# Attention into a soft mixture of experts: logits in two halves, a new order for the last batch, two more resident weight quarters

## The chip, the cores and the metric

One core of one Trainium2 chip runs the whole program. The metric is the device time of one execution in microseconds; below it is the median of three runs of the kernel before.

## What is computed

The input is `q`, `k`, `v` (8 batches, 8 heads, 576 positions, 64 channels) and forget gates `f`. Causal attention with a decay from the running sum of `log f` gives `x`, 4608 tokens of 512 channels. A soft mixture of 8 experts with 4 slots each follows:

```python
logits = x @ phi                              # 4608 x 32
d = softmax of logits over all tokens         # dispatch
slot_input = d.T @ x                          # 32 slots x 512
h = maximum(slot_input[e] @ w1[e], 0); slot_out[e] = h @ w2[e]
c = softmax of logits over the 32 slots       # combine
out = c @ slot_out                            # 4608 x 512
```

The softmax over tokens runs over the batches with a running maximum for each slot; the sums so far (`acc`) are scaled down when a batch raises it.

## The kernel before

**Loop.** The order of all instructions is written out by hand. The main loop takes one pair of heads in each step `g` from 1 to 31 (four pairs make a batch). `s1` and `tops` take row maxima of the scores two heads ahead, `mturn` and `mrows` bring them into a row of the query tile (ACT copies them to `mr`, a DMA on SP's queue moves them to `YA`, and the first `s2` matmul of the next step needs them), `s2` makes the scores again with maximum and decay subtracted, `expo` exponentiates on ACT, `causal` masks on POOL, `s3` multiplies with the values at the end of the step, and `norm` divides. `px` and `xcopy` transpose the former pair's result into a channel tile `XT`, 144 columns for each quarter of the tokens (128, and 16 of the ninth half block).

**Mixture inside the loop.** With `b, w = divmod(g - 4, 4)`, the mixture of batch `b` runs one batch behind the attention. At the end of the step with `w = 0`, `logits` makes 16 products (four pairs by four groups of 32 partitions of one PSUM tile; each is two matmul instructions). At `w = 1`, `weigh` copies them to SBUF (ACT, L386), `spread` copies the ninth block's logits to `TK` (POOL, L393), `mgroup` takes the maximum of each partition (DVE, L399), `mcast` transposes the maxima, `tokens` makes two transposes of 128 x 128 (L434), `tcopy`, `highest` and `mine` follow. At `w = 2`, `shift`, `shift2` (an exponential) and `dispatch` (L461), whose result DVE adds to `acc` (L467). `combine` prepares the second softmax. PSUM tiles named `s`, `lg`, `tk` and `ds` share three buffers; `ring` is another list of three banks, taken in turn.

**Closing stretch.** After step 31 come the last pair's `norm`, its transposes (`xt`, L334, L351), `dispatch` of batch 6, the last logits, `weigh`, `spread`, `mgroup`, `tokens`, `mcast`, `shift`, `dispatch` of batch 7, and a transpose of `acc` to `slT`. Between them stand `split` and `cols`, which cut the combine weights into a rounded part and a rest (ACT L678, DVE L680) and transpose them (PE L688) into `cT` (ACT L694). `cols(0)`, `cols(1)` and `cols(2)` run here; `cols(3)` runs among the experts.

**Experts and output.** `STEPS` orders first products (`mlp1`, L900) and second products (`mlp2`, L937) of the experts. Their weights come in 64 quarters of 512 KB. The first `NRES = 23` have SBUF tiles of their own and are loaded in loop steps 5 to 27 (`wload`). The others go through `wstream` into tiles as they fall free: query and key tiles from step 28 on, other tiles in steps 29 to 31 and in the closing stretch, and then the first quarters' own tiles. `block` multiplies `cT` with the slots' outputs (L1015), copies on ACT and DVE and writes `out` by DMA (L1021), first for the left half of the channels, between the last `mlp2`. Every DMA is issued in order on SP's queue.

Of the kernel before, what the change touches and what calls it, by code (L numbers as in the profile page):

```python
# [17 lines left out]
NS = NE * SPE  # L18
# [10 lines left out]
NRES = 23  # L29
# [43 lines left out]
def attn_softmoe(ctx: ExitStack, tc: tile.TileContext, qk, v, f, phi, w1, w2, cst, out):  # L73
# [6 lines left out]
    cs = const.tile([P, 258], F32, name="cs")  # L80
    ident, srep, ones = cs[:, 0:128], cs[:, 128:256], cs[:, 256:258]
# [18 lines left out]
    RAW = [per.tile([P, 2, S], F32, name=f"RAW{i}") for i in range(3)]  # L100
# [3 lines left out]
    XT = [per.tile([P, S], F32, name=f"XT{i}") for i in range(NPAIR)]  # L104
    V = per.tile([P, 2, NBLK, 130], F32, name="V")
    slT = per.tile([P, P], F32, name="slT")
    LD = const.tile([P, NBLK, NS], F32, name="LD")

    LGM = const.tile([P, 274], F32, name="LGM")
    LG, TK = LGM[:, 2:146], LGM[:, 146:274]  # L110
    most = [LGM[:, n : n + 1] for n in range(2)]
    fin = const.tile([P, 8], F32, name="fin")

    mk = const.tile([P, NE], F32, name="mk")
    MT = [const.tile([P, 2 * NBLK], F32, name=f"MT{i}") for i in range(3)]
# [220 lines left out]
    def channels(g):  # L336
        return XT[g % NPAIR].rearrange("p (j c) -> p j c", c=144)

    def last(g, pm, copy):

        for h in range(2):
            rows = slice(64 * h, 64 * h + 64)
            copy(channels(g)[rows, :, 128:144], pm[rows, 64 * h : 64 * h + 64].rearrange("p (j c) -> p j c", c=16))

    def xt(g, ts, copy):

        pm = turn()
        for n, t in enumerate(ts):
            turned(pm[:, 128 * n :], g, t)
        n = len([t for t in ts if t < 4])  # L350
        copy(channels(g)[:, ts[0] : ts[0] + n, 0:128], pm[:, 0 : 128 * n].rearrange("p (j c) -> p j c", c=128))  # L351
        if 4 in ts:
            last(g, pm[:, 128:256], copy)

# [40 lines left out]
    def mgroup(b):
        if not batch(b):
            return
        st["mb", b] = small.tile([P, 2], F32, name=f"mb{b}", tag="mb")
        nc.vector.tensor_reduce(st["mb", b][:, 0:1], LGM[:, 0:146], axis=AX.X, op=ALU.max)  # L399

    def mcast(b):

        if not batch(b):
            return
        pm = turn()[:, 0:128] if b == B - 1 else pv[0][:, 325:453]
        nc.tensor.transpose(pm, st["mb", b][:, 0:1].broadcast_to([P, P]), ident)
        st["cast"] = pm
# [102 lines left out]
    nc.sync.dma_start(cs, cst[:, 0:258])  # L510
# [152 lines left out]
    nc.vector.memset(TK, 0.0)  # L663
    nc.vector.memset(LGM[:, 0:2], -1.0e30)
# [33 lines left out]
    for g in range(1, NG):  # L698
# [188 lines left out]
    hs = XT[0][:, 0:512].rearrange("p (n c) -> p n c", n=2)  # L887
# [57 lines left out]
    for e, k in STEPS[:-4]:  # L945
# [140 lines left out]
```

## Time and profile before

| | us |
|---|---|
| median of three runs | 385.4 |
| lowest and highest | 384.98, 385.47 |
| the profiled execution, its own time | 385.63 |
| its span in the trace | 383.9 |
| PE busy | 361.9 (94%) |
| DVE, ACT, POOL busy | 281.6, 264.5, 262.4 |

The span runs from the first to the last instruction in the trace; 1.7 us of the execution's time lie outside it. Busy times are sums over the whole span, and a busy PE is not one at its peak. The mean granted clock of TensorE is 0.985 of full speed. The DMA queue of the hardware moved 92.73 MB.

### The profile page before, as it was taken

To read this page: it belongs to the slowest core of one execution; us is meant where nothing else is said; L and a number is where in the kernel's file an instruction comes from. 1 tells how busy PE (TensorE), PEld (TensorE's weight loads), DVE (VectorE), ACT (ScalarE), POOL (GpSimd) and SP (SyncE) were. 2 spreads that over 40 slices of the span, in tenths; PEclk is the share of its full clock that TensorE was granted. 3 is DMA by queue.
4 is the path that set the end of the run, shared out by engine and by line. 5 is a ranking of instruction groups with operands and counts; after the bars stand their busy time and mean duration, and the time that the engine had idled before them with its cause. 6 is when DMAs were issued, how large, how long until landed. Compare 5 with 4: busy or idle time off the path is not lost.

```text
span 383.9 us, 15067 instructions
## 1 busy us (share of the span) xinstructions
PE 361.9 (94%) x5777; PEld 323.2 (84%) x5777; DVE 281.6 (73%) x1133; ACT 264.5 (69%) x670; POOL 262.4 (68%) x381
## 2 busy tenths in 40 slices
PE   7999999999999999999998999999999998999850
PEld 6788999999999999999998999999999885444640
DVE  8987787889788978897888788888887543312551
ACT  8868787878787878787877787878786554011441
POOL 8797888878887888788877888888788821000000
PEclk9999999999999999999999999999999999999985
DMA  7766757677868777787777777777755999999998
GB/s 221 201 158 171 192 150 229 196 236 219 251 189 239 229 241 203 205 245 218 217 216 215 215 212 223 218 216 217 219 163 153 279 358 376 381 408 409 359 360 352
DMA packets 34052, 93.68 MB, mean 244 GB/s; under 512 B 4169, under 2 KB 9983, under 8 KB 33981
## 3 DMA queue, kind: packets, MB, share of 16 engines
q1 hardware_dynamic: 33980, 92.73, 77.1%
q8 instruction: 45, 0.74, 0.8%
q14 instruction: 27, 0.21, 0.1%
HBM read 63.93 MB, written 9.73 MB: 192 GB/s over the span
## 4 chain that ended last, share of the span: by engine, by line
PE 83%; DMA 6%; ACT 3%; DVE 3%; POOL 1%; issue 1%; SPq 0%; DVEq 0%; ACTq 0%; POOLq 0%
PE pv L308 23%; PE ring L275 14%; PE ring L276 12%; PE s L225 12%; PE pv L334 4%; PE pv L937 3%; PE lg L380 2%; PE ds L461 2%; PE pv L900 2%; PE more L900 2%; DMA YA<-mr 2%; DMA WB<-WA 1%; ACT PTS L282 1%; DMA out<-p 1%; PE more L937 1%
## 5 line engine op out<-in xcount | busy, mean ns | idle before, releaser
L282 ACT ACTIVATE PTS<-ring 128x320 f32<-128x320 f32 (+2 forms) x256 | 118.5, 502 | 47.4 <-PE ring L276 39.8
L238 DVE CUSTOM_DVE_ANT_0 s<-s,mask 128x320 f32<-128x320 f32 (+4 forms) x320 | 137.9, 451 | 6.1 <-PE s L225 1.1
L275 PE MATMUL ring<-YA,WA 67*128 67x320 f32 (+9 forms) x384 | 121.7, 329 | 1.6 <-DMA YA<-mr 1.6
L276 PE MATMUL ring<-YB,WB 128*128 128x320 f32 (+4 forms) x384 | 110.7, 296 | 0.0
L308 PE MATMUL pv<-V,PTS 128*64 128x65 f32 x3200 | 102.3, 223 | 0.9 <-POOL PTS L290 0.9
L308 PEld LDWEIGHTS pv<-V,PTS 128*64 128x64 f32 x3200 | 97.2, 138 | 4.1 <-POOL PTS L290 1.3
L225 PE MATMUL s<-WA,YA 66*128 66x288 f32 (+9 forms) x384 | 96.8, 306 | 1.4 <-ACT WA L545 0.5
L204 POOL TENSOR_TENSOR WB<-RAW,WB 64x576 fp32r<-64x576 f32 x64 | 90.5, 1415 | 7.2 <-DMA WB<-WA 2.3
L209 POOL TENSOR_TENSOR YB<-RAW,YA 64x576 fp32r<-64x576 f32 x64 | 89.7, 1421 | 2.5
L275 PEld LDWEIGHTS ring<-YA,WA 67*128 67x128 f32 (+3 forms) x384 | 69.0, 181 | 7.2 <-DMA YA<-mr 1.9
L276 PEld LDWEIGHTS ring<-YB,WB 128*128 128x128 f32 (+1 forms) x384 | 69.9, 182 | 0.0
L225 PEld LDWEIGHTS s<-WA,YA 66*128 66x128 f32 (+1 forms) x384 | 64.1, 190 | 5.9 <-DVE LGM L238 1.3
L238 DVE DVE_READ_ACCUMULATOR2_ANT MT<- 128x1 f32 x372 | 52.6, 141 | 0.0
L293 POOL TENSOR_SCALAR_AFFINE_SELECT PTS<-PTS 128x128 f32<-128x128 f32 (+1 forms) x128 | 31.5, 268 | 25.8 <-ACT PTS L282 24.2
L178 ACT CAST WA<-RAW 64x576 fp32r<-64x576 f32 x64 | 40.2, 669 | 7.9 <-DMA RAW<-in_qk 7.2
L290 POOL TENSOR_SCALAR_AFFINE_SELECT PTS<-PTS 128x384 f32<-128x384 f32 x64 | 33.4, 523 | 15.5 <-ACT PTS L282 8.4
L183 ACT CAST YA<-RAW 64x576 fp32r<-64x576 f32 x64 | 40.3, 670 | 0.5
L238 DVE CUSTOM_DVE_ANT_0 s<-s,mask,MT 128x288 f32<-128x288 f32 x62 | 32.6, 526 | 9.0
L334 PE MATMUL pv<-cs,X 128*128 128x128 f32 x155 | 37.0, 272 | 0.0
L327 DVE TENSOR_TENSOR X<-pv,rl 128x320 f32<-128x320 f32 (+1 forms) x65 | 31.6, 487 | 2.4 <-DMA V<-in_v 0.3
L322 DVE TENSOR_SCALAR rl<-pv 128x5 f32<-128x5 f32 x64 | 10.5, 164 | 27.7 <-PE pv L308 27.4
L369 ACT COPY XT<-pv 128x128 f32<-128x128 f32 (+1 forms) x93 | 24.9, 306 | 0.0
(190 smaller groups left out, 342.7 us busy)
## 6 DMA issues: line engine op xcount, KB each, us to landing
w<-in_w SPq DMA_DIRECT2D x46, 512.0 KB
RAW<-in_qk SPq DMA_DIRECT2D x31, 576.0 KB
V<-in_v SPq DMA_DIRECT2D x32, 325.0 KB
WB<-WA SPq DMA_DIRECT2D x31, 288.0 KB
YB<-YA SPq DMA_DIRECT2D x31, 288.0 KB
p<-in_w SPq DMA_DIRECT2D x7, 512.0 KB
out<-RAW SPq DMA_DIRECT2D x12, 256.0 KB
out<-p SPq DMA_DIRECT2D x5, 512.0 KB
```

Source lines behind the costliest of these rows:

```text
L178: nc.scalar.copy(WA[g % 3][0:64, S * h : S * h + S], RAW[g % 3][64:128, h])
L183: nc.scalar.copy(YA[g % 3][0:64, h, 64:640], RAW[g % 3][0:64, h])
L204: nc.gpsimd.tensor_tensor(t[0:64], RAW[g % 3][64:128, h], t[64:128].bitcast(F32), op=ALU.subtract)
L209: nc.gpsimd.tensor_tensor(YB[g % 2][64:128, h], RAW[g % 3][0:64, h], YA[g % 3][0:64, h, 64:640].bitcast(F32), op=ALU.subtract)
L225: nc.tensor.matmul(t[:, o : o + w], ya[0:m, h, 128 * blk : 128 * blk + 128], wa[0:m, j0 : j0 + w], start=True, stop=True)
L238: nc.vector.tensor_tensor_reduce(out=t[:, o : o + w], in0=t[:, o : o + w], in1=mask[:, m0 : m0 + w], scale=1.0, scalar=top if n == 3 else ...
L275: nc.tensor.matmul(o, wa[0:m, j0 : j0 + n], ya[0:m, h, 64 + i0 : 64 + i0 + w], start=True, stop=False)
L276: nc.tensor.matmul(o, wb[:, j0 : j0 + n], yb[:, h, i0 : i0 + w], start=False, stop=True)
L282: nc.scalar.activation(PT[i % 2][:, SEG_O[bank] : SEG_O[bank] + at], t[:, 0:at], AF.Exp, scale=0.125)
L290: nc.gpsimd.affine_select(d3, d3, pattern=[[0, 3], [1, 128]], compare_op=ALU.is_ge, fill=0.0, base=0, channel_multiplier=-1)
L308: nc.tensor.matmul(pvv[h][64 * u : 64 * u + 64, t, :], PT[h][:, at : at + 64], V[:, g % 2, c, 65 * h : 65 * h + 65], start=(c == 0), stop= ...
L334: nc.tensor.transpose(pm[:, 0:128], x[:, t, p % 2, 0:128], ident)
```

## The change

Only two channel tiles `XT` are left. The logits of a batch are made in two halves of two pairs each: the first half at the end of the step with `w = 2` (for the batch whose pairs are then at work), copied to SBUF by `keep` at `w = 3`; the second half at `w = 0`. `mgroup` adds the second half from PSUM to the first in SBUF and takes the maximum in the same pass on DVE. `TK` has 32 partitions instead of 128, and its transpose is 32 rows by 32 columns of identity. `mr` and other small tiles move into free corners of others, the identity's block `srep` is loaded in the closing stretch, and `NRES` is 25; `XT` becomes one more tile for `wstream`. In the closing stretch the last batch's first half has been made in step 30, its ninth block's logits of the second half are made by two more products in the layout of `TK`, dispatch of batch 6 is cut up between other matmuls, `split(1, 1)` comes later, `cols(0)` and `cols(1)` stand in other places, and `split(2)` and `cols(2)` move in among the experts, behind first products of experts 2 and 4.

```diff
-NRES = 23
+NRES = 25
...
-    cs = const.tile([P, 258], F32, name="cs")
+    cs = const.tile([P, 162], F32, name="cs")
...
+    RAWS = per.tile([P, 3, 2, S], F32, name="RAWS")
+    RAW = [RAWS[:, i] for i in range(3)]
...
-    XT = [per.tile([P, S], F32, name=f"XT{i}") for i in range(NPAIR)]
+    XT = per.tile([P, 2, S], F32, name="XT")
...
-    LG, TK = LGM[:, 2:146], LGM[:, 146:274]
+    LT = const.tile([P, 272], F32, name="LT")
+    LG, TK = LT[:, 0:144], LT[0:32, 144:272]
...
-        mr = small.tile([2 * NBLK, P], F32R, name=f"mr{g}_{h0}", tag="mr", bufs=1)
+        mr = YA[1][96 : 96 + n].rearrange("p h s -> p (h s)")[:, 0:P]
...
-    def channels(g):
-        return XT[g % NPAIR].rearrange("p (j c) -> p j c", c=144)
+    def channels(p):
+        return XT[:, p % 2].rearrange("p (j c) -> p j c", c=144)
...
-    def logits(b, *ps):
+    def logits(b, *ps, w=144, ninth=()):
...
-        if 0 in ps and b < B - 1:
-            st["lg", b] = scratch(False, f"lg{b}")
+        if b < B - 1 or 0 in ps:
+            st["lg", b] = scratch(False, f"lg{b}_{ps[0]}")
...
                 nc.tensor.matmul(
-                    plg[32 * j : 32 * j + 32, 0:144], phis[:, p, :], XT[p][:, 144 * j : 144 * j + 144], start=(p == 0), stop=(p == NPAIR - 1)
+                    plg[32 * j : 32 * j + 32, 0:w], phis[:, p, :], channels(p)[:, j, 0:w], start=(p % 2 == 0), stop=(p % 2 == 1)
                 )
+        for p in ninth:
+            both = channels(p)[:, :, 128:144].rearrange("p (o j) c -> p o j c", o=1).broadcast_to([P, 2, 4, 16])
+            nc.tensor.matmul(plg[0:32, 128:256], phis[:, p, :], both, start=(p % 2 == 0), stop=(p % 2 == 1))
-    def weigh(b):
+    def keep(b):
         if batch(b):
             nc.scalar.copy(LG, st["lg", b][:, 0:144])
...
     def mgroup(b):
...
-        nc.vector.tensor_reduce(st["mb", b][:, 0:1], LGM[:, 0:146], axis=AX.X, op=ALU.max)
+        plg = st["lg", b]
+        mb = st["mb", b] = small.tile([P, 2], F32, name=f"mb{b}", tag="mb")
+        steps = [(LG, plg[:, 0:144], most[(b - 1) % 2])]
+        if b == B - 1:
+            steps = [(LG[:, 0:128], plg[:, 0:128], most[(b - 1) % 2]), (TK, plg[0:32, 128:256], mb[0:32, 0:1])]
+        for to, new, top in steps:
+            nc.vector.tensor_tensor_reduce(
+                out=to, in0=new, in1=to, scale=1.0, scalar=top, op0=ALU.add, op1=ALU.max, accum_out=mb[0 : to.shape[0], 0:1]
+            )
...
-        for n in ns:
-            nc.tensor.transpose(st["tok", b][:, 128 * n : 128 * n + 128], (LG[:, 0:128], TK)[n], ident)
+        if 0 in ns:
+            nc.tensor.transpose(st["tok", b][:, 0:128], LG[:, 0:128], ident)
+        if 1 in ns:
+            nc.tensor.transpose(st["tok", b][:, 128:160], TK, ident[0:NS, 0:NS])
...
+    def weight(b):
+        return V.rearrange("p u t c -> p (u t c)")[:, QW : QW + NBLK * NS].rearrange("p (t s) -> p t s", t=NBLK) if b == B - 1 else LD
...
-    nc.vector.memset(TK, 0.0)
...
-        if w == 1:
-            weigh(b)
+        if w == 3:
+            keep(b + 1)
         low_q(h0 + 2)
         low_q(h1 + 2)
-        if w == 1:
-            spread(b)
+        if g == NG - 1:
+            spread(b + 1)
...
         if w == 1:
             mgroup(b)
+            spread(b)
...
         if w == 0:
-            logits(b, *range(NPAIR))
+            logits(b, 2, 3)
+        if w == 2:
+            logits(b + 1, 0, 1)
...
-    logits(B - 1, 0, 1, 2)
+    logits(B - 1, 2, w=128)
     wstream(V, PTS[:, QW : 2 * QW], PTS[:, 2 * QW : 3 * QW])
-    b = B - 1
+    b, g = B - 1, NG - 1
     ring += [ps_s.tile([P, 512], F32, name=f"more{n}", tag="s") for n in range(2)]
+    c0, c1 = (cols(n, turn) for n in range(2))
     norm(NH - 1)
+    dispatch(b - 1, 0)
+    pm = [turn(), turn(), pv[0]]
+    turned(pm[0], g, 0)
+    turned(pm[0][:, 128:], g, 4)
+    turned(pm[1], g, 2)
+    turned(pm[1][:, 128:], g, 3)
+    turned(pm[2], g, 1)
+    nc.scalar.copy(channels(g)[:, 0, 0:128], pm[0][:, 0:128])
+    nc.vector.tensor_copy(channels(g)[:, 2:4, 0:128], pm[1][:, 0:256].rearrange("p (j c) -> p j c", c=128))
+    nc.scalar.copy(channels(g)[:, 1, 0:128], pm[2][:, 0:128])
+    last(g, pm[0][:, 128:256], nc.scalar.copy, nc.vector.tensor_copy)
     split(0, 1)
-    split(1, 1)
-    dispatch(b - 1, 0, 1, 2)
-    xt(NG - 1, (0, 4), nc.scalar.copy)
-    xt(NG - 1, (2, 3), nc.vector.tensor_copy)
-    xt(NG - 1, (1,), nc.scalar.copy)
-    dispatch(b - 1, 3, 4)
-    wstream(X[0], X[1])
-    logits(b, NPAIR - 1)
-    ring.append(pv[1])
-    c0, c1, c2 = (cols(n, turn) for n in range(3))
-    weigh(b)
-    spread(b)
-    mgroup(b)
-    next(c0)
-    tokens(b, 0)
-    mcast(b)
-    highest(b)
-    next(c0)
-    tokens(b, 1)
-    tcopy(b)
-    shift(b)
-    mine(b)
-    next(c0)
-    shift2(b)
-    fade(b)
-    next(c0)
-    next(c1)
-    next(c1)
-    next(c1)
-    next(c1)
-    split(2, 0, 1)
+    dispatch(b - 1, 1)
+    logits(b, 3, w=128, ninth=(2, 3))
+    srep = XT.rearrange("p n s -> p (n s)")[:, QW : QW + 128]
+    nc.sync.dma_start(srep, cst[:, 0:128])
+    wstream(XT)
+    mgroup(b)
+    dispatch(b - 1, 2)
+    tokens(b, 0)
+    mcast(b)
+    tokens(b, 1)
+    tcopy(b)
+    highest(b)
+    shift(b)
+    shift2(b)
+    mine(b)
+    next(c0)
+    next(c0)
+    dispatch(b - 1, 3, 4)
+    wstream(X[0], X[1])
+    fade(b)
+    split(1, 1)
     dispatch(b, *range(NBLK))
     wstream(X[2], X[3])
-    next(c2)
     ps = turn()
+    next(c0)
+    next(c0)
...
-    next(c2)
-    next(c2)
-    next(c2)
+    for _ in range(4):
+        next(c1)
+    ring.append(pv[1])
...
+        if (e, k) in ((4, 0), (5, 0)):
+            for _ in cols(e - 2, turn):
+                pass
         if (e, k) == (1, 0):
             combine(b, 0)
+        if (e, k) == (2, 0):
+            split(2, 0, 1)
...
-        if (e, k) == (5, 0):
-            for _ in cols(3, turn):
-                pass
```

## Rows read from the trace of the kernel before

**Rows 1.** The page, part 4: shares of the chain that ended last, by engine.
```profile
PE 83%; DMA 6%; ACT 3%; DVE 3%; POOL 1%; issue 1%; SPq 0%; DVEq 0%; ACTq 0%; POOLq 0%
```

**Rows 2.** Busy time by stretch: stretch, its us, PE, PEld, DVE, ACT, POOL, clock, DMA share, GB/s.
```profile
290.00:300.00 10.00, 10.00 (x154) 9.74 (x154) 8.25 (x37) 6.18 (x19) 8.40 (x15) 1.00 0.59 153
336.00:338.00 2.00, 2.00 (x34) 1.01 (x30) 0.70 (x3) 0.00 (x0) 0.00 (x0) 1.00 1.03 418
364.50:365.00 0.50, 0.50 (x10) 0.47 (x8) 0.50 (x2) 0.50 (x2) 0.00 (x0) 1.00 0.37 129
```

**Rows 3.** Timeline of the SP queue, its end: start, us, issues merged.
```profile
324.55 24.23 SPq L122 DMA_DIRECT2D w<-in_w  x23
354.89 5.26 SPq L1021 DMA_DIRECT2D out<-RAW  x6
```

**Rows 4.** Timeline around the ends of loop steps 28 and 29 (start, us, what, idle before).
```profile
288.18 0.89 PEld L380 LDWEIGHTS lg<-XT,phis 128*32 128x32 f32 x32
...
289.30 0.19 PEld L275 LDWEIGHTS ring<-YA,WA 67*128 67x128 f32 x1 [0.23 <-issue]
...
289.75 0.30 DVE L399 TENSOR_REDUCE mb<-LGM 128x1 f32<-128x146 f32 x1 [0.44 <-ACT LGM L386]
...
298.27 0.19 PEld L275 LDWEIGHTS ring<-YA,WA 98*128 98x128 f32 x1
```

**Rows 5.** The chain of waits in order of time, at the two transposes of `tokens`.
```profile
292.50 0.22 PE tk L434 x2
```

**Rows 6.** Timeline of weight loads for the transposes of `cols` in the closing stretch.
```profile
319.51 0.25 PEld L688 LDWEIGHTS ring<-cs,cw 128*128 128x128 f32 x2
...
319.93 0.14 PEld L688 LDWEIGHTS ring<-cs,cw 64*128 64x128 f32 x1 [0.17 <-issue]
...
320.13 0.20 PEld L688 LDWEIGHTS more<-cs,cw 128*128 128x128 f32 x2
```

**Rows 7.** Timeline, first matmul of `s2` in loop step 31.
```profile
307.22 0.47 PE L275 MATMUL ring<-YA,WA 67*128 67x448 f32 x1 [0.37 <-DMA YA<-mr]
```

**Rows 8.** Timeline of the closing stretch, from the last `s3` to the experts.
```profile
314.68 0.65 PEld L380 LDWEIGHTS lg<-XT,phis 128*32 128x32 f32 x24
...
315.21 0.56 DVE L327 TENSOR_TENSOR X<-pv,rl 128x128 f32<-128x128 f32 x2
...
316.22 0.66 PE L334 MATMUL ring<-cs,X 128*128 128x128 f32 x4
...
318.12 0.28 ACT L386 COPY LGM<-lg 128x144 f32<-128x144 f32 x1 [0.56 <-PE lg L380]
...
318.46 0.94 POOL L393 COPY LGM<-LGM 32x32 f32<-32x32 f32 x4 [5.27 <-ACT LGM L386]
...
319.46 0.33 PE L434 MATMUL ring<-cs,LGM 128*128 128x128 f32 x1 [0.34 <-POOL LGM L393]
...
320.93 1.31 PE L461 MATMUL more<-X,LD 128*32 128x129 f32 x40
...
322.33 0.49 DVE L680 TENSOR_TENSOR cw<-ctok,cw 128x320 fp32r<-128x320 f32 x1 [1.75 <-ACT cw L678]
322.74 0.34 DVE L467 SCALAR_TENSOR_TENSOR acc<-acc,mb,more 128x129 f32<-128x129 f32 x1
...
323.85 0.81 PEld L900 LDWEIGHTS more<-w,slT 128*32 128x32 f32 x20
```

**Rows 9.** Groups of instructions on DVE by line and shape (count, busy us, mean ns).
```profile
L238 DVE DVE_READ_ACCUMULATOR2_ANT MT<- 128x1 f32 x372 | 52.6, 141 | 0.0
...
L238 DVE CUSTOM_DVE_ANT_0 s<-s,mask 128x192 f32<-128x192 f32 x64 | 23.5, 367 | 2.2
```

**Rows 10.** The chain of waits in order of time, `cols(3)` among the experts.
```profile
338.86 0.37 PE lg L688 x2
339.23 0.42 PE ring L688 x3
```

**Rows 11.** Timeline, first matmul of `s2` in loop step 20.
```profile
204.58 0.47 PE L275 MATMUL ring<-YA,WA 67*128 67x448 f32 x1 [1.21 <-DMA YA<-mr]
```

More of the change, by code (lines that the diff above doesn't have):

```diff
@@ L78, in attn_softmoe @@
     dram = ctx.enter_context(tc.tile_pool(name="dram", bufs=1, space=DRAM))
-    cs = const.tile([P, 258], F32, name="cs")
-    ident, srep, ones = cs[:, 0:128], cs[:, 128:256], cs[:, 256:258]
+    cs = const.tile([P, 162], F32, name="cs")
+    eye, ident, ones = cs[:, 0:NS], cs[:, 32:160], cs[:, 160:162]
     phis = const.tile([P, 4, NS], F32, name="phis")
@@ L99, in attn_softmoe @@
             WB[m] = fr[n].tile([P, 2 * S], F32R, name=f"WB{m}")
-    RAW = [per.tile([P, 2, S], F32, name=f"RAW{i}") for i in range(3)]
+    RAWS = per.tile([P, 3, 2, S], F32, name="RAWS")
+    RAW = [RAWS[:, i] for i in range(3)]
     PTS = per.tile([P, 3200], F32, name="PTS")
@@ L103, in attn_softmoe @@
     X = [per.tile([P, NBLK, 2, 129], F32, name=f"X{i}") for i in range(3)]
-    XT = [per.tile([P, S], F32, name=f"XT{i}") for i in range(NPAIR)]
+    XT = per.tile([P, 2, S], F32, name="XT")
     V = per.tile([P, 2, NBLK, 130], F32, name="V")
-    slT = per.tile([P, P], F32, name="slT")
     LD = const.tile([P, NBLK, NS], F32, name="LD")
-    LGM = const.tile([P, 274], F32, name="LGM")
-    LG, TK = LGM[:, 2:146], LGM[:, 146:274]
[L111 to L115, printed above, removed]
+    LT = const.tile([P, 272], F32, name="LT")
+    LG, TK = LT[:, 0:144], LT[0:32, 144:272]
+    few = const.tile([P, 18 + 6 * NBLK], F32, name="few")
+    fin, mk, top2 = few[:, 0:8], few[:, 8:16], few[:, 16:18]
+    most = [top2[:, n : n + 1] for n in range(2)]
+    MT = [few[:, 18 + 10 * i : 28 + 10 * i] for i in range(3)]
     quarter = [wres.tile([P, QW], F32, name=f"w{n}") for n in range(NRES)]
@@ L255, in mrows @@
         n = NBLK * (h1 - h0)
-        mr = small.tile([2 * NBLK, P], F32R, name=f"mr{g}_{h0}", tag="mr", bufs=1)
-        nc.scalar.copy(mr[0:n], st["pm", g, h0][0:n, 0:128])
+        mr = YA[1][96 : 96 + n].rearrange("p h s -> p (h s)")[:, 0:P]
+        nc.scalar.copy(mr, st["pm", g, h0][0:n, 0:128])
         m = TOP[g % 3]
         dst = YA[g % 3][m : m + 1, h0:h1].rearrange("c h s -> c (h s)")
-        nc.sync.dma_start(dst.bitcast(F32), mr[0:n].bitcast(F32))
+        nc.sync.dma_start(dst.bitcast(F32), mr.bitcast(F32))
     def s2(i, *which):
@@ L334, in turned, with last @@
         nc.tensor.transpose(pm[:, 0:128], x[:, t, p % 2, 0:128], ident)
-    def channels(g):
-        return XT[g % NPAIR].rearrange("p (j c) -> p j c", c=144)
-    def last(g, pm, copy):
+    def channels(p):
+        return XT[:, p % 2].rearrange("p (j c) -> p j c", c=144)
+    def last(g, pm, *copies):
         for h in range(2):
             rows = slice(64 * h, 64 * h + 64)
[L343 to L353, printed above, removed]
+            copies[h % len(copies)](channels(g)[rows, :, 128:144], pm[rows, 64 * h : 64 * h + 64].rearrange("p (j c) -> p j c", c=16))
     TURN = {0: (0, 0), 1: (1, 0), 2: (1, 128), 4: (1, 325), 3: (0, 128)}
@@ L392, in spread @@
                 part = LG[32 * j : 32 * j + 32, 128:144].rearrange("p (o c) -> p o c", o=1).broadcast_to([32, 2, 16])
-                nc.gpsimd.tensor_copy(TK[0:32].rearrange("p (o c) -> p o c", o=2)[:, :, 16 * j : 16 * j + 16], part)
+                nc.gpsimd.tensor_copy(TK.rearrange("p (o c) -> p o c", o=2)[:, :, 16 * j : 16 * j + 16], part)
     def mgroup(b):
@@ L417, in mine @@
             return
-        own = small.tile([P, NS], F32, name=f"own{b}", tag="own", bufs=1)
         nc.vector.tensor_tensor_reduce(
-            out=own, in0=under, in1=srep[:, 0:NS], scale=1.0, scalar=0.0, op0=ALU.mult, op1=ALU.add, accum_out=most[b % 2]
+            out=st["cast"][:, 0:NS], in0=under, in1=eye, scale=1.0, scalar=0.0, op0=ALU.mult, op1=ALU.add, accum_out=most[b % 2]
         )
@@ L445, in shift @@
         top = under.rearrange("p (o s) -> p o s", o=1).broadcast_to([P, NBLK, NS])
-        nc.vector.tensor_tensor(LD, ctok[:, b], top, op=ALU.subtract)
+        nc.vector.tensor_tensor(weight(b), ctok[:, b], top, op=ALU.subtract)
     def shift2(b):
         if batch(b):
-            nc.scalar.activation(LD, LD, AF.Exp)
+            nc.scalar.activation(weight(b), weight(b), AF.Exp)
     def dispatch(b, *ts):
@@ L460, in dispatch @@
                 x = xtile(b, j // 2)[:, t, j % 2]
-                nc.tensor.matmul(ds[32 * j : 32 * j + 32, 0:129], LD[:, t, :], x, start=(t == 0), stop=(t == NBLK - 1))
+                nc.tensor.matmul(ds[32 * j : 32 * j + 32, 0:129], weight(b)[:, t, :], x, start=(t == 0), stop=(t == NBLK - 1))
         if NBLK - 1 not in ts:
@@ L497, in warm @@
             to = pv[1][:, 326 : 326 + w] if a is cs else ring[0][:, 0:w]
-            nc.tensor.matmul(to, a[:, 0:128], a[:, 0:w], start=True, stop=True)
+            nc.tensor.matmul(to, a[:, 0:128], a[:, 0 : w // 2].rearrange("p (o c) -> p o c", o=1).broadcast_to([P, 2, w // 2]), start=True, stop=True)
     lane = slice(64, 128)
@@ L886, in attn_softmoe @@
     PH = {}
-    hs = XT[0][:, 0:512].rearrange("p (n c) -> p n c", n=2)
+    hs = (
+        V.rearrange("p u t c -> p (u t c)")[:, QW : QW + 256].rearrange("p (a c) -> p a c", a=2),
+        RAWS.rearrange("p n h s -> p n (h s)")[:, 0:2, QW : QW + 128],
+    )
     def rest(n):
@@ L904, in relu @@
     def relu(e):
-        to, scale = hs[:, e // 2 % 2], mk[:, e : e + 1]
+        to, scale = hs[e // 2 % 2], mk[:, e : e + 1]
+        ph = PH[e][:, 0:256].rearrange("p (a c) -> p a c", a=2)
         if e % 2 == 0:
-            nc.vector.tensor_scalar(to, PH[e][:, 0:256], scale, 0.0, op0=ALU.mult, op1=ALU.max)
+            nc.vector.tensor_scalar(to, ph, scale, 0.0, op0=ALU.mult, op1=ALU.max)
         else:
-            nc.vector.scalar_tensor_tensor(to, in0=PH[e][:, 0:256], scalar=scale, in1=to, op0=ALU.mult, op1=ALU.max)
+            nc.vector.scalar_tensor_tensor(to, in0=ph, scalar=scale, in1=to, op0=ALU.mult, op1=ALU.max)
     def blank_h(e):
@@ L919, in own @@
         for c in range(2):
-            nc.tensor.transpose(pm[:, 128 * c : 128 * c + 128], hs[:, e // 2 % 2, 128 * c : 128 * c + 128], ident)
+            nc.tensor.transpose(pm[:, 128 * c : 128 * c + 128], hs[e // 2 % 2][:, c], ident)
         for n in (e, e + 1):
@@ L1060 @@
     cst = np.ones((P, 714), np.float32)
-    cst[:, 0:128] = np.eye(P)
-    cst[:, 128:256] = np.tile(np.eye(NS), (4, 4))
+    cst[:, 128:256] = np.eye(P)
+    cst[:, 0:128] = np.tile(np.eye(NS), (4, 4))
     cst[:, 258:578] = 0
```

8 lines of the change are left out of this document (4 added, 4 removed).

## The prediction

> **What bounds the kernel now.** I read the chain that ended last first, for the engine on which the time lies: PE holds 83% of it [rows 1]. The next best, DMA with 6%, stands mostly at the end. So up to the last products a microsecond of PE is a microsecond of time, and another engine counts only where PE waits for it. I then read the busy time by stretch, to see whether DMA could be a second bound. In step 29 its share is 0.59, with room; among the experts it is 1.03 at 418 GB/s, the queue always full. SP issues the last 23 weight loads in 24.2 us, one each 1.05, and the first output at 354.89 [rows 3]. For half a microsecond, at 364.5, the share falls to 0.37 [rows 2]. That dip is the important row: the left half's output has drained and the right half's is not yet made. After it the queue has only output to write, so the end comes a fixed time after PE, ACT and DVE deliver the right half's first block. PE's chain sets the end; the stream of weights runs beside it with little to spare. The timeline gives the durations, PE's weight loads above all: their starts show gaps that the overlapping matmuls hide.
>
> **Two more resident quarters, two channel tiles.** Two loads move to steps 28 and 29. They stand on SP's queue behind the loads of values and of queries and keys; behind them the step's `mr` transfer comes some microseconds later. The cover is the 0.41 of free DMA share in step 29 [rows 2], and steps 5 to 27 already carry such a load. Without that cover a 512 KB load costs 1.25 us at 418 GB/s. The stream that fills the queue at the end gets two quarters shorter, 2.5 us of DMA. By the dip this is worth nothing alone; it makes the dip longer. What it does is let the queue follow if PE gets earlier. I take 0. Other storage (`mr` inside `YA`, `few`, the identity in other columns, `srep` loaded late, 64 KB or 0.15 us of a queue that is ahead) changes no count of instructions on PE: 0. Bounds for all of these: 0 to +0.5 us.
>
> **Logits in halves.** The count of products is the same, but the engine goes over to them twice for a batch instead of once. 32 loads take 0.89 us and 24 take 0.65 [rows 4, 8], so one costs 0.03. From the first load to the first of `s2` are 1.12 us; 32 x 0.03 are 0.96. So 0.16 is the price of leaving the logits; the load of `s2` has waited 0.23 there, and none stands at the end of step 29, where `s3` goes straight into `s2` [rows 4]. A half costs 16 x 0.03 + 0.16 = 0.64, two cost 1.28 instead of 1.12: +0.16 for each of batches 0 to 6, together **+1.1 us**. Bounds: 0, if the wait overlaps work that I do not see, and 7 x 0.23 = +1.6.
>
> The other engines do not feel it. `keep` is the copy that `weigh` was, at the start of a step, before anything for ACT to do. `mgroup` becomes a pass of DVE that waits for PE alone; queued behind it are `tops`, and the PSUM buffer that it frees. Before, it waited 0.44 for ACT's copy [rows 4], so it ends no later. `spread` now waits for DVE behind POOL's subtractions, with `causal` behind it; POOL is no part of the chain there. DVE and POOL are free enough: 0.
>
> **The transpose of `TK`.** In the loop two full transposes take 0.22 us of the chain, 0.11 each [rows 5]. Now the second has 32 rows and 32 columns. No row shows 32 rows, but `cols` has transposes with 64: the load of such a one comes 0.20 after full ones that are 0.11 apart, with a wait of 0.17 that no other engine explains, and the full one behind it again 0.20 later [rows 6]. So a change of the rows in use costs 0.09 in and 0.09 out. I take this nearest row: +0.18 for each of seven batches, **+1.3 us**. Lower bound: no change-over, and 32 columns instead of 128 save three quarters of 0.11, 7 x 0.08 = -0.6. Upper bound: the whole wait of 0.17 on both ways, 7 x 0.26 = +1.8.
>
> The Trainium skill (TensorEngine Tiling (Array Packing), Key Properties) says that changing the tiling mode drains TensorE. For 64 rows the trace agrees (0.20 against 0.11); for 32 rows nothing here shows it. By that rule the sum would be the one I make, and without it 1.9 us less.
>
> **Step 30.** The last batch's first half is made there: 0.64 us. PE idles 0.37 us behind it, for the `mr` transfer [rows 7], so **+0.3 us**. `keep` and `spread` of this half run in step 31 in the shadow of that start.
>
> **The closing stretch.** Before, PE makes 24 + 24 small matmul instructions after the last `s3`, and the transposes start at 316.22, though `norm` has ended at 315.77 [rows 8]. Now 8 + 8 stand there, some 0.5 us, and the transposes start with `norm`'s halves: 0.45 earlier. The copies are shared between ACT and DVE, and `dispatch` of batch 6 no longer stands between them and the logits; I put the end of the logits 0.7 earlier, at 317.4 where ACT started at 318.12. The two extra products cost 4 x 0.03, and DVE must do `split(0, 1)` (0.49) before `mgroup`; both fit. Then ACT's copy and POOL's 0.94 led to the second transpose of `tokens` at 319.46, 1.34 later [rows 8]. Now two dependent passes of DVE do it, each at most 0.37 + 0.14 [rows 9], and the transposes of the maxima and of `TK` follow: 318.55, 0.9 earlier. `dispatch` of batch 7 then could start 0.9 earlier, at 320.0; it reuses the bank of batch 6's sums, which DVE reads (0.34) behind `shift` and `mine` until about then. That is the wait that is late next. After it, DVE added the sums at 322.74, 0.5 after the last matmul, since `split(2, 1)` (0.49) stood in front [rows 8]; this has moved away, 0.45 earlier. From there to the experts (323.85) nothing shrinks; the five transposes of `cols(1)` fit beside the copy of `slT`. Together **-1.4 us**, between -0.9 (if the copies gain nothing) and -1.8.
>
> **`cols(2)` among the experts.** Its five transposes now stand in a part where PE is never idle. `cols(3)` paid 0.37 + 0.42 = 0.79 there [rows 10]; behind `own` the engine is in the right shape already, so down to 5 x 0.11 = 0.55. I take **+0.65 us**. `split(2)` costs ACT and DVE half a microsecond each, which idle there.
>
> **Sum.** 1.1 + 1.3 + 0.3 - 1.4 + 0.65 = +1.95 us on the profiled execution's 385.63 (span 383.9 and 1.7 outside). That execution lies 0.2 above the median of 385.4; from the median, 387.3.
>
> **Rivals.**
>
> *The change-overs are not paid.* One mechanism, on the other side: if PE fills the gaps between array shapes from its queue, the split costs 0, the small transpose saves 0.6, step 30 costs 16 x 0.03 - 0.37 = 0.1, and with -1.4 and +0.65 the sum is -1.25: 384.2. It decides as soon as split and small transpose together cost less than some 0.02 us a batch. For it: PE's rows are modelled in part. Against it: the waits of 0.23 and 0.17 [rows 4, 6].
>
> *Only 32 rows are free.* The split costs 1.1, the transpose saves 0.6: 385.4, no change.
>
> *DMA sets the end.* Then two quarters less give -2.5 where I count -1.4 + 0.65 + 0.3, and the loop's +2.4 remains, since the stream starts where the loop ends: 385.3, no change. The full queue [rows 2] speaks for it, the dip at 364.5 against it. The Trainium skill (DMA: Bandwidth & Descriptors, Specifications) gives 435 GB/s as the ceiling of the fabric; by that the two quarters would be an estimated 2.4 us. The trace agrees, with 418.
>
> *A late `mr` transfer, more often.* Once the first `s2` of a step waited 1.21 us for it [rows 11]; only one or two steps in 31 had such a wait. Other phases of the queue, with two loads more, could hit two more steps: +2.4, 389.7. Against it: steps 28 and 29 look like those before them.
>
> **How the numbers follow.** Forecast, change-overs as measured: 0.50, 386.4 to 388.2. Late transfers: 0.08. Only 32 rows free: 0.19. DMA: 0.08. No change-over: 0.15. 0.2% is about 0.8 us, and less cannot be told from no change. So slower 0.58, same 0.27, faster 0.15. The forecast's own bounds (all of them high: +0.5, +0.5, +0.5 and +0.5, not at once) reach 388.6; to the other side the range takes in the two cases of no change and half of the last: 384.6.
>
> **What would show it.** In the trace after: from `s3` to `s3` a batch of four steps takes 0.34 us more; the load of `s2` waits behind logits at two steps of four; the load behind the small transpose comes 0.2 later; the experts start 1.4 us earlier counted from the last `s3`, and `cols(2)` takes 0.55 to 0.8 there; the dip in DMA share before the right half is longer. The forecast is wrong if the batch keeps its length, or if the closing stretch gains far from 1.4.

## The result: slower by 0.7%

The changed kernel takes 387.99 us (median of 4 runs, 387.89 to 388.24), the one before 385.32 (384.98 to 385.47): ratio 1.0071, 95% interval 1.0054 to 1.0089. Forecast were 387.3 in a range of 384.6 to 388.6. The medians are 2.7 us apart; the profiled span, on which the terms are read below, grew by 2.3, from 383.9 to 386.2 us. The sum was nearly met, but not all of its terms were; the rest of the text takes it apart.

PE still holds the chain that ended last (page, part 4; [rows 1]):

```profile
PE 82%; DMA 6%; DVE 3%; ACT 3%; issue 1%; SPq 1%; POOL 1%; DVEq 0%; ACTq 0%; POOLq 0%
```

**The loop.** PE's weight loads at the end of step 26 (a first half), and behind the end of step 28 (a second half) with the transposes of `tokens` that follow; the last row is POOL's `spread`:

```profile
272.21 0.40 PEld L368 LDWEIGHTS lg<-XT,phis 128*32 128x32 f32 x16
272.84 0.19 PEld L274 LDWEIGHTS ring<-YA,WA 98*128 98x128 f32 x1 [0.23 <-issue]
...
290.19 0.40 PEld L368 LDWEIGHTS lg<-XT,phis 128*32 128x32 f32 x16
290.82 0.19 PEld L274 LDWEIGHTS ring<-YA,WA 67*128 67x128 f32 x1 [0.23 <-issue]
...
293.76 0.14 PEld L433 LDWEIGHTS tk<-cs,LT 128*128 128x128 f32 x1
294.06 0.13 PEld L435 LDWEIGHTS tk<-cs,LT 32*128 32x128 f32 x1 [0.17 <-POOL LT L385]
294.24 0.19 PEld L274 LDWEIGHTS ring<-YA,WA 67*128 67x128 f32 x1
...
293.01 0.93 POOL L385 COPY LT<-LT 32x32 f32<-32x32 f32 x4
```

The wait of 0.23 behind logits, once in four steps before [rows 4], stands twice now, and the first load of `s2` comes 0.63 us behind the first of the logits each time. The load of the 32-row transpose comes 0.30 behind the full one and `s2` 0.18 behind that: 0.48, where two full ones take 0.22 [rows 5]. But the view names another cause for that wait: `spread`, which ends at 293.94, 0.12 ahead of the load. That is the first dispute for the experiments.

**Step 31.** The first matmul of `s2` behind the half of step 30; PE had idled 0.37 us there before [rows 7]. The last row is the load of weights for that matmul in the kernel before:

```profile
308.59 0.70 PE L368 MATMUL lg<-XT,phis 128*32 128x144 f32 x16
310.02 0.47 PE L274 MATMUL ring<-YA,WA 67*128 67x448 f32 x1 [0.74 <-DMA YA<-YA]
...
307.22 0.19 PEld L275 LDWEIGHTS ring<-YA,WA 67*128 67x128 f32 x1 [0.51 <-DMA YA<-mr]
```

The half's 0.63 us should have covered that wait. The transfer came later still, and another 0.74 us stand behind the logits.

**The closing stretch**, from the last `s3` to the experts ([rows 8]; weight loads and matmuls, DVE and ACT):

```profile
317.36 0.16 PEld L368 LDWEIGHTS lg<-XT,phis 128*32 128x32 f32 x8
...
318.24 0.70 PE L333 MATMUL ring<-cs,X 128*128 128x128 f32 x4 [0.23 <-DVE X L326]
...
319.75 0.49 DVE L683 TENSOR_TENSOR cw<-ctok,cw 128x320 fp32r<-128x320 f32 x1
...
319.90 0.27 PE L373 MATMUL lg<-XT,phis 128*32 128x128 f32 x1
...
320.27 0.35 DVE L397 CUSTOM_DVE_ANT_0 LT<-lg,LT,few 128x128 f32<-128x128 f32 x1
...
321.43 0.24 PE L435 MATMUL more<-cs,LT 32*128 32x32 f32 x1
...
322.39 0.34 ACT L454 ACTIVATE V<-V 128x160 f32<-128x160 f32 x1 [0.39 <-DVE V L450]
...
322.71 0.35 DVE L471 SCALAR_TENSOR_TENSOR acc<-acc,mb,ring 128x129 f32<-128x129 f32 x1 [0.19 <-PE ring L465]
322.89 0.30 ACT L424 ACTIVATE mb<-few 128x1 f32<-128x1 f32 x1
...
323.21 1.31 PE L465 MATMUL ring<-X,V 128*32 128x129 f32 x40 [0.59 <-ACT mb L424]
...
324.66 0.35 DVE L471 SCALAR_TENSOR_TENSOR acc<-acc,mb,ring 128x129 f32<-128x129 f32 x1 [1.20 <-PE ring L465]
...
325.96 0.16 PEld L913 LDWEIGHTS ring<-w,LD 128*32 128x32 f32 x8
```

From the first logits to the experts it is 8.60 us; it was 9.17 [rows 8]. That gains 0.57 us, where 1.4 were forecast. The largest loss stands at `dispatch` of batch 7: its exponentials are ready at 322.73, and it starts at 323.21. The row names ACT's `fade`. The sums of batch 6, which DVE reads until 323.06 from the bank that `dispatch` writes next, would explain it too: the second dispute.

**Experts and output.** The chain of waits among the experts (`cols(2)` behind an `own`, L934, then `cols(3)`), and busy time by stretch (columns as in [rows 2]):

```profile
333.59 3.43 PE pv L951 x32
...
338.75 0.37 PE pv L934 x2
339.12 0.22 PE lg L691 x2
339.33 0.42 PE more L691 x3
...
341.62 0.37 PE more L691 x2
341.99 0.42 PE pv L691 x3
342.41 3.57 PE pv L951 x32
```

```profile
357.00:359.00 2.00, 2.00 (x32) 1.22 (x30) 1.03 (x3) 0.96 (x4) 0.00 (x0) 1.00 0.04 17
370.00:372.00 2.00, 1.66 (x12) 1.00 (x10) 0.60 (x2) 1.17 (x2) 0.00 (x0) 1.00 1.09 384
```

`cols(2)` costs 0.22 + 0.42 = 0.64. The dip in DMA share is now two whole microseconds at 0.04, since the weights are all there before the first output is.

### The profile page after: what moved, and what is told of

It is laid out like the page before. It is cut to its first block, busy times and chain, and to the rows that moved or that the text cites. A ratio compares the mean times of both kernels' runs of the same rounds, so it can differ in the third digit from the quotient of the medians.

```text
span 386.2 us, 15104 instructions
## 1 busy us (share of the span) xinstructions
PE 363.6 (94%) x5781; PEld 321.9 (83%) x5781; DVE 284.1 (74%) x1143; ACT 268.5 (70%) x669; POOL 262.7 (68%) x381
## 4 chain that ended last, share of the span: by engine, by line
PE 82%; DMA 6%; DVE 3%; ACT 3%; issue 1%; SPq 1%; POOL 1%; DVEq 0%; ACTq 0%; POOLq 0%
PE pv L307 23%; PE ring L274 14%; PE ring L275 12%; PE s L224 12%; PE pv L333 4%; PE ring L913 4%; PE pv L951 3%; PE lg L368 2%; PE ds L465 2%; DMA p<-in_w 2%; DMA WB<-WA 1%; DMA out<-p 1%; ACT PTS L281 1%; PE ring L951 1%; DMA YA<-YA 1%
## 5 line engine op out<-in xcount | busy, mean ns | idle before, releaser
L203 POOL TENSOR_TENSOR WB<-RAWS,WB 64x576 fp32r<-64x576 f32 x64 | 90.5, 1414 | 7.2 <-DMA WB<-WA 2.3
L208 POOL TENSOR_TENSOR YB<-RAWS,YA 64x576 fp32r<-64x576 f32 x64 | 89.9, 1423 | 2.5
L237 DVE DVE_READ_ACCUMULATOR2_ANT few<- 128x1 f32 x372 | 52.7, 142 | 0.0
L177 ACT CAST WA<-RAWS 64x576 fp32r<-64x576 f32 x64 | 40.2, 669 | 5.1 <-DMA RAWS<-in_qk 4.4
L182 ACT CAST YA<-RAWS 64x576 fp32r<-64x576 f32 x64 | 40.3, 671 | 0.5
L237 DVE CUSTOM_DVE_ANT_0 s<-s,mask,few 128x288 f32<-128x288 f32 x62 | 32.6, 526 | 8.9
```

The source lines that it names most:

```text
L177: nc.scalar.copy(WA[g % 3][0:64, S * h : S * h + S], RAW[g % 3][64:128, h])
L182: nc.scalar.copy(YA[g % 3][0:64, h, 64:640], RAW[g % 3][0:64, h])
L203: nc.gpsimd.tensor_tensor(t[0:64], RAW[g % 3][64:128, h], t[64:128].bitcast(F32), op=ALU.subtract)
L208: nc.gpsimd.tensor_tensor(YB[g % 2][64:128, h], RAW[g % 3][0:64, h], YA[g % 3][0:64, h, 64:640].bitcast(F32), op=ALU.subtract)
L237: nc.vector.tensor_tensor_reduce(out=t[:, o : o + w], in0=t[:, o : o + w], in1=mask[:, m0 : m0 + w], scale=1.0, scalar=top if n == 3 else ...
```

## The experiments

For each kernel the table has the length of step 21 (w = 1) and step 23 (w = 3) and the start of the last `s3` matmul, then the us from there to the experts' first product, from that to the second product of `slots(1)` (the sum over slots of the right half), and from that to the end of the span; each worked out from starts in the profile. Steps with w = 2 and w = 0 do not differ, but for late `mr` transfers. a_best2 is not in it: its profile has a mean granted clock of 0.94, where the others have 0.98 to 0.99.

| kernel | step 21 | step 23 | last s3 | to experts | to slots | to end | ratio to before (interval) |
|---|---|---|---|---|---|---|---|
| before | 10.09 | 8.69 | 314.53 | 9.32 | 37.44 | 22.6 | 1 |
| changed | 9.87 | 9.29 | 317.21 | 8.75 | 38.11 | 22.1 | 1.0071 (1.0054 to 1.0089) |
| a_spread | 9.87 | 9.30 | 316.47 | 8.75 | 38.09 | 22.2 | 1.006 (1.004 to 1.008) |
| a_full | 9.66 | 9.29 | 315.20 | 8.54 | 38.11 | 22.2 | 1.0018 (1.0002 to 1.0033) |
| a_spread_full | 9.60 | 9.30 | 315.57 | 8.54 | 38.09 | 22.2 | 1.0002 (0.9984 to 1.0021) |
| b_small | 10.36 | 8.69 | 315.63 | 9.22 | 38.04 | 22.9 | 1.0052 (1.0033 to 1.0071) |
| a_rows64 | 9.89 | 9.29 | 316.98 | 8.79 | 38.11 | 22.1 | 1.0067 (1.0044 to 1.0089) |
| a_res23 | 9.87 | 9.30 | 316.73 | 8.86 | 38.11 | 22.2 | 1.0045 (1.0016 to 1.0074) |
| a_whole | 10.35 | 8.69 | 316.04 | 8.76 | 38.11 | 22.7 | 1.0042 (1.0014 to 1.0071) |
| a_tail | 9.87 | 9.30 | 316.75 | 8.32 | 37.14 | 22.1 | 0.9999 (0.9970 to 1.0027) |
| a_pad | 9.88 | 9.31 | 316.73 | 8.76 | 38.11 | 22.7 | 1.0091 (1.0055 to 1.0127) |
| a_best1 | 9.60 | 9.29 | 315.12 | 8.26 | 37.15 | 22.2 | 0.9956 (0.9928 to 0.9984) |
| a_best3 | 10.09 | 8.67 | 313.93 | 8.27 | 37.30 | 22.8 | 0.9981 (0.9966 to 0.9996) |

**`spread` or the change of rows?** In the changed kernel, at w = 1 (a_spread):

```
-        low_q(h1 + 2)
+        if w != 1:
+            low_q(h1 + 2)
...
         if w == 1:
             mgroup(b)
             spread(b)
+            low_q(h1 + 2)
```

> The changed kernel with `spread` (POOL) moved ahead of the second of the two subtractions of a step with w = 1. In the changed kernel the load of the 32-row transpose starts 0.30 us behind the load of the full one, and `spread` ends 0.12 before that load. Theory A (the forecast's: the price is the change-over of rows in use): the 0.30 stays, four steps still take 37.73 us, 388.0 us in all. Theory B (the transpose waits for `spread`, which PE reaches earlier since only half of the logits stand ahead of it): the 0.30 falls to 0.11, four steps take about 37.54, 0.19 x 7 = 1.3 us are gained, 386.7 us in all.

Then `TK` with 128 partitions, zeros below 32 (a_full), and both edits (a_spread_full):

```
+    TKF = LT[:, 144:272]
...
-            nc.tensor.transpose(st["tok", b][:, 128:160], TK, ident[0:NS, 0:NS])
+            nc.tensor.transpose(st["tok", b][:, 128:256], TKF, ident)
```

> The changed kernel with `TK` at 128 partitions again (zeros below 32) and its transpose 128 by 128; `spread` stays where it is. Theory A (change-over of rows): both loads around the transpose come 0.11 behind the ones before them, 0.26 less in four steps, 1.8 us in all, 386.2 us. Theory B (wait for `spread`): the load of the second transpose still comes 0.30 behind the first, and only the 0.07 behind it goes: 0.5 us in all, 387.5 us.

> Both edits. Theories A and B expect the same here: no wait and no change-over, loads 0.11 apart, four steps 37.47 us, 386.2 us in all. If something else stands behind the 0.26 us for four steps (a third cause), it is left over here.

Weight loads behind step 28, and POOL's `spread`, with `spread` moved:

```profile
293.84 0.14 PEld L433 LDWEIGHTS tk<-cs,LT 128*128 128x128 f32 x1
294.14 0.13 PEld L435 LDWEIGHTS tk<-cs,LT 32*128 32x128 f32 x1 [0.17 <-issue]
294.32 0.19 PEld L274 LDWEIGHTS ring<-YA,WA 67*128 67x128 f32 x1
...
291.75 0.96 POOL L385 COPY LT<-LT 32x32 f32<-32x32 f32 x4
```

`spread` now ends 1.4 us ahead of the load, and nothing moved: only the name behind the wait changed, from POOL to "issue". The same loads with the full transpose alone, and with both edits:

```profile
292.75 0.14 PEld L433 LDWEIGHTS tk<-cs,LT 128*128 128x128 f32 x1
292.98 0.14 PEld L435 LDWEIGHTS tk<-cs,LT 128*128 128x128 f32 x1
292.98 0.25 PEld L274 LDWEIGHTS ring<-YA,WA 67*128 67x128 f32 x1
```

```profile
293.21 0.14 PEld L433 LDWEIGHTS tk<-cs,LT 128*128 128x128 f32 x1
293.32 0.14 PEld L435 LDWEIGHTS tk<-cs,LT 128*128 128x128 f32 x1
293.43 0.19 PEld L274 LDWEIGHTS ring<-YA,WA 67*128 67x128 f32 x1
```

So the 0.26 us for four steps are the change-over (step 21 from 9.87 to 9.60). Theory B had hold of something too: with full transposes `spread` makes the second load wait some 0.1 us (step 21 is 0.06 to 0.09 longer than with both edits). In the changed kernel this wait lies under the other. PE reaches the place earlier than before, with half of the logits ahead of it; `spread` before ended 0.5 us ahead of need.

The small transpose alone, in the kernel before (b_small):

```
-    LG, TK = LGM[:, 2:146], LGM[:, 146:274]
+    LG, TK = LGM[:, 2:146], LGM[0:32, 146:274]
...
+                nc.tensor.transpose(st["tok", b][:, 128:160], TK, ident[0:NS, 0:NS])
```

> The kernel before with the 32-row `TK` and its 32 x 32 identity alone. There `spread` ends 0.50 us before the load of the transpose. Theory A: +0.18 to +0.26 for four steps, 1.3 to 1.8 us in all, ratio 1.0034 to 1.0047. Theory B: the load comes 0.11 behind the first transpose, only the load of `s2` behind it is late by 0.07, or by nothing: 0 to +0.5 us, ratio 1.000 to 1.0013.

Step 21 grows by 0.27, as theory A has it, though `spread` has time to spare there (it ends 0.7 us ahead of the load). The span loses 0.8 us more than the loop does, and 0.6 of that among the experts. The chain of waits there:

```profile
344.23 1.73 PE more L903 x32
345.95 0.04 PE ring L923
346.00 10.16 DMA w<-in_w
356.16 0.04 issue
```

The last weights land at 356.16, and PE waits for them (37.44 to 38.04 from the experts to `slots`). So the stream of weights runs close behind PE's chain in the kernel before.

With 64 rows instead of 32, and `spread` moved (a_rows64):

```
+    TKF = LT[0:64, 144:272]
...
-            nc.tensor.transpose(st["tok", b][:, 128:160], TK, ident[0:NS, 0:NS])
+            nc.tensor.transpose(st["tok", b][:, 128:192], TKF, ident[0:64, 0:64])
```

> The run with `spread` moved, and `TK` at 64 partitions (zeros in 32 to 63), its transpose 64 x 64. With 32 rows the load of the small transpose comes 0.31 us behind the full one and the load of `s2` 0.17 behind it, 0.48 together where full transposes take 0.22. The forecast took its price from `cols`, where a load of 64 rows comes 0.20 behind a full one and the next 0.20 behind that. Theory A1 (the number of rows sets the price): with 64 rows 0.20 and 0.20 here too, 0.40 together, 0.08 less for four steps, 0.6 us in all. Theory A2 (the place sets it: behind a load in flight and ahead of `s2`): 0.31 and 0.17 again, the same time as the run with `spread` moved, 387.5 us.

```profile
294.32 0.14 PEld L433 LDWEIGHTS tk<-cs,LT 128*128 128x128 f32 x1
294.63 0.13 PEld L435 LDWEIGHTS tk<-cs,LT 64*128 64x128 f32 x1 [0.17 <-issue]
294.83 0.19 PEld L274 LDWEIGHTS ring<-YA,WA 67*128 67x128 f32 x1
```

0.31 in and 0.20 out. The time stays that of a_spread, as A2 has it, but not for A2's reason, since the premise of both theories is a misreading. The row of `cols` at 319.51 [rows 6] merges two full loads, and the second of them, taken alone, stands here ahead of the load of 64 rows:

```profile
319.62 0.14 PEld L688 LDWEIGHTS ring<-cs,cw 128*128 128x128 f32 x1
319.93 0.14 PEld L688 LDWEIGHTS ring<-cs,cw 64*128 64x128 f32 x1 [0.17 <-issue]
```

So the load of 64 rows comes 0.31 behind a full one in `cols` too, not 0.20, and the next one, at 320.13, 0.20 behind it. The price is the same in both places: 0.31 in with 64 rows and with 32, and out again 0.20 with 64 rows and 0.17 with 32.

**Resident quarters** (a_res23):

```
-NRES = 25
+NRES = 23
```

> The changed kernel with 23 resident quarters instead of 25. In the changed kernel the DMA queue stands still for 2.1 us at 357 to 359, when the last weights have landed, and two quarters are 2.5 us of DMA. Theory A (the forecast's: the resident quarters are worth nothing): the idle 2.1 us fill up and no more than 0.4 us of wait for weights appears on PE; 388.0 to 388.4 us. Theory B (the stream of weights sets the end): +2.5 us, 390.5 us.

The experts take the same 38.11 us, and the DMA share at 357 to 359 goes from 0.04 to 0.80. In this kernel the two quarters are worth nothing, as the forecast had it.

**Whole logits** (a_whole: 23 quarters, `XT` with four tiles):

```
-            logits(b, 2, 3)
-        if w == 2:
+            logits(b, 0, 1, 2, 3)
+        if g == NG - 2:
             logits(b + 1, 0, 1)
```

> The changed kernel with four channel tiles, 23 resident quarters and the logits of batches 0 to 6 whole, behind the step with w = 0, with ACT's copy ahead of the maxima; the last batch stays in halves. To be held against the run with 23 quarters. Theory A (a half pays 0.14 to 0.16 us for leaving the products): four steps fall from 37.73 to 37.59 us, 0.9 to 1.1 us are gained up to the last `s3`, apart from late `mr` transfers. Rival (products of 32 columns cost the same wherever they stand, and the 0.37 us for four steps are all from the transpose): four steps keep their length.

Step 21 takes 0.48 more, step 23 0.61 less: the split costs 0.13, and the same in a_best3 against a_best1 (0.49 and 0.62). The gain up to the last `s3`, against a_res23, is 0.7 us, and the end takes 0.6 of it back (22.16 to 22.73).

**The bank and `cols(3)`** (a_tail):

```
     split(1, 1)
+    turn()
     dispatch(b, *range(NBLK))
...
+    c3 = cols(3, turn)
     gathered(1)
+    next(c3)
     slots(1)
+    next(c3)
+    next(c3)
     halve(1)
+    next(c3)
```

> Two edits behind the last `s3` of the changed kernel. First, `dispatch` of batch 7 gets another PSUM bank than that of batch 6. Theory A: what holds it is DVE's addition of batch 6's sums, which ends 323.06; with another bank it starts when the exponentials are there (322.73), 0.3 to 0.4 us earlier than 323.21. Rival: it waits for ACT's `fade`, as the view of waits names it, and starts when it did. Second, `cols(3)` moves from the experts into the two waits of PE around the sum over slots of the right half (0.48 and 0.86 us): 0.7 to 0.8 us less from the first expert to that sum, nothing given back. Together 386.8 us; 387.2 if the rival is right.

```profile
321.92 0.34 ACT L454 ACTIVATE V<-V 128x160 f32<-128x160 f32 x1 [0.39 <-DVE V L450]
...
322.41 0.30 ACT L424 ACTIVATE mb<-few 128x1 f32<-128x1 f32 x1
...
322.31 1.31 PE L465 MATMUL ring<-X,V 128*32 128x129 f32 x40 [0.16 <-ACT V L454]
```

`dispatch` starts 0.05 behind the exponentials and ahead of `fade`: it was the bank, and the name in the row was wrong. That is 0.43 us. Moving `cols(3)` gave 0.97; 0.79 are its transposes, as in [rows 10], and 0.14 more the products behind them (3.57 us in the chain above, where 3.43 stand without `cols` ahead).

**The end** (a_pad):

```
+    per.tile([P, 8], F32, name="pad")
     RAWS = per.tile([P, 3, 2, S], F32, name="RAWS")
```

From `slots` to the end the changed kernel takes 0.5 us less than before, and a_whole gave that back:

> The changed kernel with 32 unused bytes ahead of the staging tile of queries and keys, from which most of the output is written. Its address is then no multiple of 64 bytes, as in the kernel before and in the run with four channel tiles. From the second sum over slots to the end of the span the changed kernel takes 0.5 us less than the kernel before, and its queue moves 381 GB/s at 369 to 373 us where the run with four channel tiles moves 346. Theory A (the address of the source sets that rate): about 345 GB/s there, 0.5 to 1.1 us longer than the changed kernel from that sum to the end. Rival (the rate hangs on something else, such as when the writes meet): no change, 388.0 us.

The stretches in this run (384 and 383 GB/s in the changed kernel):

```profile
370.00:372.00 2.00, 1.02 (x8) 0.64 (x6) 0.56 (x1) 1.06 (x2) 0.00 (x0) 1.00 1.02 343
372.00:374.00 2.00, 1.48 (x7) 0.62 (x7) 0.82 (x2) 0.88 (x2) 0.00 (x0) 1.00 1.01 341
```

Moving the tile by 32 bytes changes the rate, and costs 0.6 us at the end. (The unused bytes also move `p0` and `p2`, the other tiles that output is written from; most of these four microseconds are written from `RAWS`.) That a multiple of 64 bytes is enough, as the expectation has it, is not so; a_best3 below shows it.

**Together.** a_best1 has the full transpose and the edits of a_spread and a_tail; a_best2 one more unused tile behind, which moves `p0` and `p2` by 32 bytes; a_best3 the full transpose, the edits of a_tail and those of a_whole:

> The full transpose, `spread` ahead of the second subtraction, and both edits behind the last `s3`, together: the 385.3 us of the run with the first two, less 0.4 and 0.75, 384.2 us: ratio 0.997 to the kernel before. If the stream of weights (2.1 us of slack in the changed kernel, whose experts start 1.9 us later) sets the end instead, 385.0.

> The best version so far (384.2 us) with 32 unused bytes behind the staging tiles, which bring the other tiles that the output is written from (p0, p2) to multiples of 64 bytes too. If the address sets the rate: two microseconds of writing at 340 GB/s go at 380, 0.2 us less, 384.0 us. Otherwise 384.2 us.

> The best version with the logits of batches 0 to 6 whole: four channel tiles, 23 resident quarters, the full transpose, both edits behind the last `s3`, and the addresses of the run with them. PE: 0.11 us less for four steps, 0.8 us up to the last `s3`, 383.4 us. The stream of weights has two quarters more to bring (2.5 us) and stood still for about 1.8 us in the best version: if it sets the end, 384.1 us or more.

a_best1 takes 384.21 us, as forecast, and beats both kernels. a_best2 has 383.89 (ratio 0.9975, 0.9953 to 0.9996): no difference that this can tell. a_best3 reaches the last `s3` 1.2 us earlier than a_best1 (0.8 by the split, the rest by late `mr` transfers) and is no faster. Two things stand against that gain, and this run does not part them. From 352 to 364 its DMA share is 1.02 (0.82 in a_best1): with the two quarters more to bring, the queue has no gap left. And the end is 0.7 us longer, where a_pad lost 0.6 by its addresses alone. Those of a_best3 are not as good as a_best1's, though the expectation takes them to be: it stores `LT` and `top2` in one tile, `LM`, which is 64 bytes longer than `LT`, and so `RAWS` stands 64 bytes off. Writing from `RAWS`, first in a_best1, then in a_best3:

```profile
366.00:368.00 2.00, 2.00 (x16) 1.49 (x13) 0.96 (x2) 1.39 (x3) 0.00 (x0) 1.00 1.09 383
...
366.00:368.00 2.00, 1.76 (x8) 0.82 (x8) 0.78 (x2) 1.15 (x2) 0.00 (x0) 1.00 1.02 349
```

## Why the prediction held, and where it did not

| term | forecast | in the profile | shown by |
|---|---|---|---|
| logits in halves | +1.1 | 7 x 0.12 = +0.8 | a_whole, a_best3; 0.60 - 0.22 - 0.26 (steps 23 and 21, transpose) |
| 32-row transpose in the loop | +1.3 | 7 x 0.26 = +1.8 | a_spread_full, b_small |
| step 30 | +0.3 | +0.88 | 7.90 to 8.78 us for step 31 |
| closing stretch | -1.4 | -0.57 | a_tail, a_full |
| `cols(2)` | +0.65 | +0.67 | 37.44 to 38.11 |
| other storage, the end | 0 | -0.5 | a_pad |
| late `mr` and single steps | 0 | -0.8 | the rest up to the last `s3` |

These come to +2.3 us, the growth of the span; forecast were 1.95. That the sum is so near is in part luck: three terms came out 1.9 us higher than forecast and three 1.6 us lower. By its own sign, that the closing stretch gains far from 1.4, the forecast was wrong there. The mechanisms of the first two terms were right: PE pays for leaving the 32-column products and for changing the rows in use, and a batch takes 0.38 us more (steps 21 to 24), where 0.34 were forecast. The Trainium skill (TensorEngine Tiling (Array Packing), Key Properties) has the mode change drain the engine; the runs agree for 32 rows, with 0.48 us against 0.22.

- *The small transpose* was mis-sized: 0.26 for four steps, at the upper bound, instead of 0.18. The nearest row was the right one, but it was misread: 0.20 for the way in comes out only if the row at 319.51 held a third load, at 319.73, and it holds two. Read rightly, `cols` gives 0.31 + 0.20 - 0.22 = 0.29, what the loop pays with 64 rows (a_rows64), and 0.03 more than with 32. The closing stretch pays for it too (0.21, from 8.75 to 8.54 in a_full), which the forecast left out.
- *"The other engines do not feel it"* is only nearly true: `spread` is late by 0.1 us, under the dearer wait.
- *The closing stretch* failed at its own "wait that is late next". The forecast saw the bank and put its release at the moment when `dispatch` needed it. It cost 0.43. `split(0, 1)` in front of `mgroup` does fit: the maxima's pass starts right behind it, at 320.27, and the last product of the logits ends only at 320.17. Even so the second transpose comes 0.71 earlier rather than 0.9, though the first transposes gained 0.66 where 0.45 were said. `cols(1)` does not fit beside the copy of `slT`: from the last sum to the experts it is 1.30 us instead of 1.11.
- *Step 30*: 0.88 in this profile, but step 31 takes 7.96 to 8.06 in the other runs of changed kernels, so the half itself is all but hidden (+0.06). The forecast set its 0.64 against the 0.37 that PE's products idled; the load of weights had idled 0.51 there. The rest is one late transfer.
- *Late `mr` transfers*, the rival: there are two in the profile, as before, in step 31 and once more (0.79 us in step 8, where it was 1.21 in step 20), and one of about 1 us in most of the other runs. Not more often. What delays each was not settled.
- *DMA* does not set the end of this kernel (a_res23). But b_small shows it close behind in the kernel before, so the quarters may be worth something once PE is faster. a_best1 with 23 quarters and the same addresses would show it; that was not run.
- *Storage at 0* was wrong: the new addresses give back half a microsecond, and the forecast's bounds for it had only a loss.
- *The rival without change-overs* has a slip: by its own sum, to come out faster by 0.2% split and small transpose together would have to save some 0.02 us a batch, not cost less than that.

## What to carry to other kernels

A row that merges several instructions has the start of the first alone: look at its count before you take a price from the distance to the next row, or narrow the window until each stands alone. Here that was 0.11 us, a third of the way in. A name behind a wait is a candidate, and two waits can lie one under the other: move the named work away and look whether the start moves. Before shortening a chain of small steps, write down when each PSUM bank that it reuses is read for the last time.

## What the hardware showed unasked

Writing 1 KB packets from SBUF, the queue full, ran at 383 GB/s from a tile whose address is a multiple of 256 bytes and at 342 from the same tile 32 bytes further (a_pad). In a_best3, where the tile stands 64 bytes past such a multiple, it ran at 349. (The addresses are those in the built programs.) The weights went the same way at 340 to 345 us: 416 GB/s into tiles at multiples of 256 bytes (changed kernel), 405 into tiles 32 bytes short of one (kernel before), 409 into tiles 64 bytes past one (a_best3). No run changed that by itself. No tile here stands at a multiple of 128 bytes that is none of 256, so which of the two counts stays open. a_best2 brought only `p0` to such a multiple (`p2` is 64 bytes short of one), and did not come out measurably faster.
